# ScalarE's order in a top-k attention with a gated feed-forward: exponentials, evictions and sines by kind of slot

## The chip, the cores and the metric

The kernel runs on one core of one Trainium2 chip. The metric is the device time of one execution in microseconds (us). Before the change it is 1595.27 us, the median of three runs (1594.74 to 1595.98); the profiled execution has a span of 1596.1 us. Engines are named as in the profile: PE is TensorE (PEld its weight loads), DVE is VectorE, ACT is ScalarE, POOL is GpSimd, SP is SyncE.

## What is computed

An attention block that keeps the 32 largest scores of each row, and behind it a feed-forward with the gate h·cos(h). All of it is float32.

```python
# q, k, v: (B, H, S, D) = (8, 8, 576, 64);  w_in: (512, 2048);  w_out: (2048, 512)
scores = q @ k.T / sqrt(D)                       # per batch and head, 576 x 576
kth    = the 32nd largest of each row
scores = where(scores >= kth, scores, -1e9) - rowmax
attn   = exp(scores); attn /= attn.sum(-1) + 1e-9
x      = (attn @ v), heads side by side          # (4608, 512)
h      = x @ w_in
out    = (h * cos(h)) @ w_out                    # (4608, 512)
```

## The kernel before

The work is cut into 144 units: 36 tiles of 128 tokens, with four pairs of heads each. A tile of tokens with its four units feeds one block of the feed-forward. One pass of the main loop, a slot, starts the top-k of unit `u` and carries older units on: `w` is one slot older (its mask and exponentials), `x` two (normalised on POOL, split into halves and written to DRAM), `y` three (transposed by DMA), and `z` is a pair of units whose product with v is taken in every odd slot. Scores of the next units are made ahead: in most odd slots those of two units (`made` has two entries), in most even slots none. In a tile that lies across two batches (units 16 to 19, 52 to 55, 88 to 91 and 124 to 127) each unit's scores are made alone, one per slot.

```python
def slot(i, u, w, x, y, z):
    if x:
        reciprocal(x)              # DVE, waits for x's row sums
    if u:
        topk_first(u, w)           # DVE: two folds of u's scores, the last merges of w, round 0
        decode_second(2)
    if u:
        topk_round(u, 1); topk_round(u, 2); topk_round(u, 3)      # DVE
    if z:
        values(z)                  # PE: attn @ v of two units, into a PSUM tile
    made = scored.get(i, [])
    if not made or not z:
        feed(1)                    # PE: feed-forward tasks
    for m in made:
        scores(m)                  # PE
    if w:
        bounds(w)                  # ACT, waits for DVE's merges of w
        mask(w)                    # ACT, two Prelu over 128x576
    take_banks()                   # ACT: evictions of full feed-forward banks
    if z:
        take_values(z)             # ACT: xT, the feed-forward's input
    take_scores(units[i + 1])      # ACT: PSUM scores to SBUF
    if w:
        exponentials(w)            # ACT: two Exp with row sums, then den
    ...                            # loads, transposes(y)
    gate(1)                        # POOL: g = h * cos
    if x:
        normalise(x); split(x); write_halves(x)                   # POOL, SP
    feed(2)
    take_banks()
    ...
    reduce_first(); reduce_second()                               # POOL: argument of the cosine
    feed(3)
    sines(2)                       # ACT: cosine as a sine
```

Each engine carries its instructions out in this order. `feed(n)` puts up to `n` tasks of the feed-forward on PE, if the credit allows it. A task is a half of a bank with `w_in` (`ff1`) or a quarter of one with `w_out` (`ff2`: two of eight products into one bank); a block has eight of each. The kinds alternate two by two.

```python
ff["credit"] = min(ff["credit"] + 5.0 - 0.9 * len(scored.get(i, [])), 5.3)     # each slot
...
def open_bank():
    if ff["open"] + len(full) == 2:     # the feed-forward has two PSUM banks
        take_banks()
    ff["open"] += 1

def take_first(blk, g, mm, half):       # an ff1 bank: line 478
    nc.scalar.mul(out=g[:, half * 512 : half * 512 + 512], in_=mm, mul=INV_2PI)
    if half == 1:
        fresh.append([blk, g])

def take_second(blk, i, o):             # an ff2 bank: line 553
    ob = ffw.tile([P, DM], F32, tag="ob", name="ob")
    nc.scalar.mul(out=ob, in_=o, mul=2.0 * math.pi)
    nc.scalar.dma_start(out=out[row : row + P, :], in_=ob)
...
def sines(least):
    n = sum(c[3] < ff["now"] for c in waiting)          # reduced in an earlier slot
    if n == 0 or (n < least and waiting[0][3] + 2 > ff["now"]):
        return
    ...                                                  # Sin of each, line 523

def exponentials(u):                                     # line 334
    for j in range(2):
        nc.scalar.activation(out=s[:, j], in_=s[:, j], func=AF.Exp, bias=nd[:, j : j + 1],
                             scale=1.0, accum_out=den[:, j : j + 1])
    nc.scalar.activation(out=den, in_=den, func=AF.Identity, bias=eps, scale=1.0)
```

Exp and Sin need different activation tables, so a change from one to the other brings an ACT_TABLE_LOAD with it.

Of the kernel before, what the change touches and what calls it, by code (L numbers as in the profile page):

```python
# [31 lines left out]
def kernel(  # L32
# [52 lines left out]
    for i in range(DF // CW):  # L85
        w = consts.tile([P, NC, CW], F32, tag=f"w_in{i}", name=f"w_in{i}")
# [4 lines left out]
    for f in range(NF):  # L91
        w = consts.tile([P, DM], F32, tag=f"w_out{f}", name=f"w_out{f}")
# [38 lines left out]
    def decode_second(n):  # L131


        for _ in range(min(n, len(wq["second"]))):
            st, w = wq["second"].popleft()
            wi = w.bitcast(I32)
            nc.vector.tensor_scalar(out=w, in0=w, scalar1=2.0, scalar2=None, op0=ALU.max)
            nc.vector.tensor_scalar(
                out=wi, in0=wi, scalar1=3, scalar2=None, op0=ALU.logical_shift_left
            )  # L140
            wq["third"].append((st, w))
# [71 lines left out]
    def scores(u):  # L213
        sc = u["sc"] = ps.tile([P, 2, 512], F32, tag="sc", name="sc", bufs=2)
        for to, k0, k1 in ((sc, 0, SB), (sc_ends[u["n"] % 2], SB, S)):
            for j in range(2):
                d = slice(j * D, (j + 1) * D)
                for b, q0, rows, r0 in u["parts"]:
                    st = pairs[b, u["hp"]]
                    nc.tensor.matmul(  # L220
                        to[r0 : r0 + rows, j, 0 : k1 - k0],
                        st["q"][d, q0 : q0 + rows],
                        st["k"][d, k0:k1],
                        start=True,
                        stop=True,
                    )
# [30 lines left out]
    def topk_first(u, w):  # L257

        u["top"] = tops[u["n"] % len(tops)]
        merges = [merge_first, merge_second] if w and w["folds"] else []  # L260
        if u["folds"]:
            for op in (ALU.max, ALU.min):
                fold(u, op)
                if merges:
                    merges.pop(0)(w)
        else:
            u["rest"] = work.tile([P, 2, S], F32, tag="rest", name="rest", bufs=1)
        for merge in merges:
            merge(w)
        topk_round(u, 0)  # L270

    def topk_round(u, rnd):
        top, rest, lasts = u["top"], u["rest"], TOPK // 8 - 1
        end = TOPK - 1 - 8 * rnd
        at = top[:, :, end : end - 8 if rnd < lasts else None : -1, 0]
        if u["folds"]:
            search(at, rest[:, :, 0:HS], rest[:, :, 0:HS], rnd < lasts)
            if rnd < TOPK // 16:

                low = top[:, :, 1 + 8 * rnd : 9 + 8 * rnd, 1]  # L280
                search(low, rest[:, :, HS:S], rest[:, :, HS:S], rnd < TOPK // 16 - 1)
        else:
            search(at, u["s"] if rnd == 0 else rest, rest, rnd < lasts)
        if rnd == lasts:
            del u["rest"]
# [36 lines left out]
    def mask(u):  # L322

        s, nb = u["s"], u.pop("nb")
        for j in range(2):
            nc.scalar.activation(  # L326
                out=s[:, j], in_=s[:, j], func=AF.Prelu, bias=nb[:, j, 1:2], scale=SCALE, alpha=FAR
            )

    def exponentials(u):  # L330
        s, nd = u["s"], u.pop("nd")
        den = u["den"] = small.tile([P, 2], F32, tag="den", name="den")
        for j in range(2):
            nc.scalar.activation(  # L334
                out=s[:, j], in_=s[:, j], func=AF.Exp, bias=nd[:, j : j + 1], scale=1.0,
                accum_out=den[:, j : j + 1],
            )

        nc.scalar.activation(out=den, in_=den, func=AF.Identity, bias=eps, scale=1.0)  # L339

    def reciprocal(u):
        u["rden"] = small.tile([P, 2], F32, tag="rden", name="rden")
        nc.vector.reciprocal(u["rden"], u.pop("den"))  # L343
# [106 lines left out]
    def ff1(blk, i):  # L450
        w = blk["w"]
        nf = 256 // w
        part = i % 4
        if part == 0:
            blk["g"].append(ffw.tile([P, 1024], F32, tag="g", name="g", bufs=CHUNKS))
            ff["live"] += 1
        if part % 2 == 0:
            open_bank()
            blk["mm"] = ps.tile([P, 512], F32, tag="mm", name="mm", bufs=2)
        g, mm = blk["g"][-1], blk["mm"]  # L460
        for a in range(nf):
            f = i * nf + a
            at = (part % 2 * nf + a) * w
            for c in range(NC):
                nc.tensor.matmul(  # L465
                    mm[:, at : at + w],
                    w_in[f // FC][:, c, (f % FC) * P : (f % FC + 1) * P],
                    blk["xT"][:, c],
                    start=c == 0,
                    stop=c == NC - 1,  # L470
                )
        if part % 2 == 0:
            return
        ff["open"] -= 1
        full.append((take_first, blk, g, mm, part // 2))
# [6 lines left out]
    def take_banks():  # L482
        while full:
            take, *what = full.popleft()
            take(*what)
# [30 lines left out]
    def sines(least):  # L516

        n = sum(c[3] < ff["now"] for c in waiting)
        if n == 0 or (n < least and waiting[0][3] + 2 > ff["now"]):
            return  # L520
        for _ in range(n):
            blk, g, x, _, scale = waiting.popleft()
            nc.scalar.activation(out=x, in_=x, func=AF.Sin, bias=halfpi, scale=scale)  # L523
            sined.append((blk, g, x))
# [8 lines left out]
    def ff2(blk, i, f0):  # L533
        w = blk["w"]
        if f0 == 0:
            open_bank()
            blk["o"] = ps.tile([P, 512], F32, tag="mm", name="o2", bufs=2)
        o = blk["o"]
        per = 1024 // w
        for f in range(f0, f0 + 2):  # L540
            g = blk["g"][f // per]
            at = (f % per) * w + i * P
            nc.tensor.matmul(  # L543
                o, g[:, at : at + P], w_out[f], start=f == 0, stop=f == NF - 1
            )
        if f0 + 2 < NF:
            return
        ff["open"] -= 1
        full.append((take_second, blk, i, o))
# [25 lines left out]
    def feed(n):  # L575

        ff["tick"] += 1
        while n > 0 and ff["credit"] >= 1:
            for kind in (ff["kind"], 1 - ff["kind"]):
                if (can_first, can_second)[kind]():  # L580
                    break
            else:
                return
            if kind == 0:
                ff1(*first.popleft())
            else:
                ff2(*second.popleft())
            if kind != ff["kind"] or ff["half"]:
                ff["kind"], ff["half"] = 1 - kind, 0
            else:  # L590
                ff["half"] = 1
            n, ff["credit"] = n - 1, ff["credit"] - 1
# [8 lines left out]
    EARLY, LAST = 2 * NP, NU - NP  # L601
# [9 lines left out]
    for n in range(NP, len(order)):  # L611
        i = last[order[n - 5]] if n >= 5 else 0
        at_slot.setdefault(max(i, NP + 2), []).append((load_qk, *order[n]))
        i = last_values[order[n - 6]] if n >= 6 else 0
# [51 lines left out]
    def slot(i, u, w, x, y, z):  # L666
        if x:
            reciprocal(x)
        if u:
            topk_first(u, w)  # L670
            decode_second(2)
        if u:
            topk_round(u, 1)
            topk_round(u, 2)
            topk_round(u, 3)
        if z:
            values(z)
        made = scored.get(i, [])
        if not made or not z:
            feed(1)  # L680
        for m in made:
            scores(m)

        if w:
            bounds(w)
            mask(w)
        take_banks()
        if z:
            take_values(z)
        take_scores(units[i + 1])  # L690
        if w:
            exponentials(w)
        for load, b, hp in at_slot.get(i, []):
            load(b, hp)
        load_weights(2)
        if y:
            transposes(y)
        gate(1)
        if x:
            normalise(x)  # L700
            split(x)
            write_halves(x)
        feed(2)
        take_banks()
        decode_third()
        decode_first(2)
        reduce_first()
        reduce_second()
        feed(3)
        sines(2)  # L710

    def last_slot(i, u, w, x, y, z):
        if x:
# [48 lines left out]
    for i in range(NU + 1):  # L762
# [4 lines left out]
        u, w = (units[i - n] if 0 <= i - n < NU else None for n in range(2))  # L767
        x, y = (units[i - n] if EARLY <= i - n < LAST else None for n in range(2, 4))
        z = units[i - 5 : i - 3] if i % 2 and EARLY <= i - 5 < LAST else None
# [53 lines left out]
```

## Time and profile before

| engine | busy us | share of the span | instructions |
|---|---|---|---|
| PE | 1446.7 | 91% | 10360 |
| DVE | 1418.5 | 89% | 4689 |
| ACT | 1154.5 | 72% | 2322 |
| POOL | 1104.6 | 69% | 838 |

Two engines are near their whole span, and a third is far from it. The page's busy time is an average over a start (up to about 250 us, in which the weights are decoded), the long regular middle (to about 1475 us) and an end in which only the feed-forward is left: from 1500 us on DVE is busy 28.71 of 96 us, PE 91.67. In a list of waits, a line such as "DVE rden L343 <- ACT den L339" says which instruction stood idle and what let it go. A line of the timeline has the start, the duration, the engine, the line of code, the operation with output and input, the number of instructions merged, and in brackets the idle time ahead and its releaser.

### The profile page before, as it was taken

The numbers are of one execution on the slowest core, as the hardware profiler recorded it, in microseconds if no ns is written. First come the engines' busy times: TensorE is split into PE (matmuls) and PEld (weight loads), VectorE is DVE, ScalarE is ACT, GpSimd is POOL, SyncE is SP. The second block draws the span as 40 slices with busy tenths as digits, with TensorE's granted clock in tenths as the row PEclk, the third lists the DMA queues.
The fourth block names the chain that finished last, engine by engine and source line by source line (L and its number), as shares of the span: only waits on it lengthen the run. The fifth ranks groups of instructions, "written<-read, shape, count | busy, mean of one in ns | idle before, by whom it ended". The sixth has DMA issues, their size and how long they took to land.

```text
span 1596.1 us, 30173 instructions
## 1 busy us (share of the span) xinstructions
PE 1446.7 (91%) x10360; PEld 1041.4 (65%) x10360; DVE 1418.5 (89%) x4689; ACT 1154.5 (72%) x2322; POOL 1104.6 (69%) x838
## 2 busy tenths in 40 slices
PE   4568789999999999999999999999999999999999
PEld 2455467667676666766666666676766666767675
DVE  7999999998999998999999999999999999998821
ACT  7887666767777777777777777777777777777741
POOL 4687867866777777777777776777777767777610
PEclk6678799999999999999999999999999999999999
DMA  8423365545544465445564455644554445544300
GB/s 266 142 81 83 111 185 135 131 136 158 166 122 117 125 171 153 129 126 155 156 156 126 126 141 156 165 125 147 155 156 126 108 131 155 141 126 112 89 14 14
DMA packets 371753, 212.20 MB, mean 133 GB/s; under 512 B 321296, under 2 KB 337936, under 8 KB 371600
## 3 DMA queue, kind: packets, MB, share of 16 engines
q1 hardware_dynamic: 366192, 200.63, 45.7%
q10 hardware_dynamic: 5408, 9.65, 1.7%
q8 instruction: 81, 1.33, 0.3%
q14 instruction: 72, 0.59, 0.1%
HBM read 45.09 MB, written 87.29 MB: 83 GB/s over the span
## 4 chain that ended last, share of the span: by engine, by line
PE 39%; ACT 23%; DVE 20%; POOL 11%; issue 4%; DMA 2%; SPq 1%; DVEq 0%; ACTq 0%; POOLq 0%
PE mm L465 15%; PE o L543 12%; PE rim L408 6%; DVE top L304 6%; DVE rest L244 6%; ACT s L334 5%; DVE rest L307 5%; ACT s L326 5%; PE sc L220 4%; POOL g L530 3%; POOL halves L360 3%; ACT s L230 2%; ACT L334 2%; POOL s L348 2%; ACT nd L317 2%
## 5 line engine op out<-in xcount | busy, mean ns | idle before, releaser
L304 DVE MAX8 top<-rest 128x8 f32<-128x288 f32 (+1 forms) x1656 | 681.5, 460 | 0.0
L465 PE MATMUL mm<-xT,w_in 128*128 128x128 f32 x4608 | 586.7, 287 | 64.6 <-ACT g L478 56.6
L465 PEld LDWEIGHTS mm<-xT,w_in 128*128 128x128 f32 x4608 | 561.1, 201 | 122.2 <-ACT g L478 80.5
L543 PE MATMUL o<-w_out,g 128*128 128x512 f32 x1152 | 522.4, 596 | 6.1 <-POOL w_out L148 4.0
L307 DVE MATCH_REPLACE8 rest<-top,rest 128x288 f32<-128x288 f32 (+1 forms) x1104 | 494.9, 456 | 0.0
L543 PEld LDWEIGHTS o<-w_out,g 128*128 128x128 f32 x1152 | 208.8, 191 | 218.1 <-issue 208.0
L360 POOL COPY halves<-s 128x2304 uint16<-128x2304 uint16 x132 | 277.6, 2103 | 96.0 <-DMA rows<-halves 91.4
L348 POOL TENSOR_SCALAR s<-s,rden 128x576 f32<-128x576 f32 x288 | 212.0, 748 | 79.4 <-DVE rden L343 79.2
L334 ACT ACTIVATE s<-s,nd 128x576 f32<-128x576 f32 x288 | 221.1, 771 | 0.8
L504 POOL TENSOR_SCALAR x<-g 128x1024 f32<-128x1024 f32 x68 | 71.1, 1046 | 202.1 <-ACT g L478 202.1
L326 ACT ACTIVATE s<-s,nb 128x576 f32<-128x576 f32 x288 | 205.4, 760 | 0.0
L244 DVE TENSOR_TENSOR rest<-sc,s 128x576 f32<-128x576 f32 x264 | 198.6, 753 | 3.6 <-DVE rden L343 0.6
L408 PEld LDWEIGHTS rim<-pT,v 128*64 128x64 f32 x2560 | 136.4, 142 | 78.8 <-ACT nb L314 22.7
L408 PE MATMUL rim<-pT,v 128*64 128x128 f32 (+1 forms) x2560 | 164.7, 274 | 23.5 <-ACT pT L389 13.4
L530 POOL TENSOR_TENSOR g<-g,x 128x1024 f32<-128x1024 f32 x68 | 160.7, 2365 | 16.0 <-ACT x L523 16.0
L513 POOL TENSOR_TENSOR x<-g,x 128x1024 f32<-128x1024 f32 x68 | 161.3, 2372 | 5.7
L220 PE MATMUL sc<-k,q 64*128 64x448 f32 (+1 forms) x640 | 149.8, 591 | 14.5 <-DMA k<-in_k_dram 8.7
L314 ACT ACTIVATE nb<-top 128x4 f32<-128x4 f32 x144 | 29.3, 204 | 171.5 <-DVE top L297 171.0
L478 ACT ACTIVATE g<-mm 128x512 f32<-128x512 f32 x144 | 83.7, 583 | 84.4 <-PE mm L465 84.4
L230 ACT COPY s<-sc 128x896 f32<-128x896 f32 x144 | 129.3, 898 | 6.8 <-PE sc L220 6.8
L343 DVE RECIPROCAL rden<-den 128x2 f32<-128x2 f32 x144 | 22.5, 156 | 111.2 <-ACT den L339 110.0
L414 ACT COPY xT<-rim 128x256 f32<-128x256 f32 (+1 forms) x78 | 27.6, 354 | 119.6 <-PE rim L220 105.5
(55 smaller groups left out, 1339.1 us busy)
## 6 DMA issues: line engine op xcount, KB each, us to landing
rows<-halves SPq DMA_DIRECT2D x132, 576.0 KB, 3.2
out_dram<-ob ACTq DMA_DIRECT2D x36, 256.0 KB, 2.4
q<-in_q_dram SPq DMA_DIRECT2D x31, 288.0 KB, 3.1
st<-in_moe_w_in_dram SPq DMA_DIRECT2D x16, 512.0 KB, 5.4
v<-in_v_dram SPq DMA_DIRECT2D x32, 256.0 KB, 3.2
st<-in_moe_w_out_dram SPq DMA_DIRECT2D x16, 512.0 KB, 3.5
k<-in_k_dram SPq DMA_DIRECT2D x31, 144.0 KB, 3.4
k<-in_k_dram SPq DMA_DIRECT2D x32, 128.0 KB, 4.0
```

The lines of the kernel that those rows point to most:

```text
L220: nc.tensor.matmul(to[r0 : r0 + rows, j, 0 : k1 - k0], st["q"][d, q0 : q0 + rows], st["k"][d, k0:k1], start=True, stop=True,)
L244: nc.vector.tensor_tensor(out=u["rest"][:, :, i * HS : (i + 1) * HS], in0=sc[:, :, 0:HS], in1=s[:, :, HS:S], op=op,)
L304: nc.vector.max(to[:, j], src[:, j])
L307: nc.vector.match_replace(rest[:, j], to[:, j], src[:, j], NEG)
L326: nc.scalar.activation(out=s[:, j], in_=s[:, j], func=AF.Prelu, bias=nb[:, j, 1:2], scale=SCALE, alpha=FAR)
L334: nc.scalar.activation(out=s[:, j], in_=s[:, j], func=AF.Exp, bias=nd[:, j : j + 1], scale=1.0, accum_out=den[:, j : j + 1],)
L348: nc.gpsimd.tensor_scalar(out=s[:, j], in0=s[:, j], scalar1=rden[:, j : j + 1], scalar2=1.0, op0=ALU.mult, op1=ALU.mult,)
L360: nc.gpsimd.tensor_copy(out=halves, in_=s.rearrange("p (k h) -> p h k", h=2))
L408: nc.tensor.matmul(o[d, to], lhsT, rhs, start=c == 0, stop=c == NT)
L465: nc.tensor.matmul(mm[:, at : at + w], w_in[f // FC][:, c, (f % FC) * P : (f % FC + 1) * P], blk["xT"][:, c], start=c == 0, stop=c == NC - 1,)
L530: eng.tensor_tensor(out=g, in0=g, in1=x, op=ALU.mult)
L543: nc.tensor.matmul(o, g[:, at : at + P], w_out[f], start=f == 0, stop=f == NF - 1)
```

## The change

It changes the order in which ACT takes its work, by the kind of slot. In an odd slot in which scores of two units are made (`late`), the exponentials come right behind the mask, ahead of the evictions of the feed-forward's bank, of xT and of the scores. In a slot in which no scores are made, a full bank is taken first of all, before the bounds that wait for DVE. Sines are issued in odd slots only, as soon as one is ready; in even slots only near the start and the end. And a `late` slot ends with one task of the feed-forward at most, not three. It is meant to keep DVE from waiting for row sums behind work that waits for PE, and PE from waiting for a bank behind work that waits for DVE.

```diff
         for m in made:
             scores(m)
 
+
+        late = z and len(made) == 2
+        if not made:
+            take_banks()
         if w:
             bounds(w)
             mask(w)
+        if w and late:
+            exponentials(w)
         take_banks()
         if z:
             take_values(z)
         take_scores(units[i + 1])
-        if w:
+        if w and not late:
             exponentials(w)
         for load, b, hp in at_slot.get(i, []):
             load(b, hp)
@@
         reduce_first()
         reduce_second()
-        feed(3)
-        sines(2)
+        feed(1 if late else 3)
+        if i % 2:
+            sines(1)
+        elif i < EARLY + 8 or i > LAST - 2:
+            sines(2)
```

`EARLY` is 8 and `LAST` is 140.

## Prediction

> **What bounds the kernel now.** I read the page first: busy times, then the costliest groups. No engine is the bound alone.
>
> ```profile
> PE 1446.7 (91%) x10360; PEld 1041.4 (65%) x10360; DVE 1418.5 (89%) x4689; ACT 1154.5 (72%) x2322; POOL 1104.6 (69%) x838
> ...
> PE 39%; ACT 23%; DVE 20%; POOL 11%; issue 4%; DMA 2%; SPq 1%; DVEq 0%; ACTq 0%; POOLq 0%
> ...
> L465 PE MATMUL mm<-xT,w_in 128*128 128x128 f32 x4608 | 586.7, 287 | 64.6 <-ACT g L478 56.6
> ```
>
> The chain that ended last changes engines all the time, and ACT, busy only 72%, holds 23% of it: it carries the waits from one near-full engine to the other. So the list of waits comes next, for 400 to 1450 us (the regular middle).
>
> ```profile
> ACT nb L314 <- DVE top L297: 121.2, 77, 1.9
> ACT xT L414 <- PE rim L220: 83.0, 48, 3.1
> ...
> DVE rden L343 <- ACT den L339: 72.8, 28, 3.8
> PEld mm L465 <- ACT g L478: 66.5, 26, 2.8
> ACT g L478 <- PE mm L465: 49.2, 26, 2.6
> PE mm L465 <- ACT g L478: 46.8, 26, 1.9
> ```
>
> In these 1050 us are some 26 blocks of four slots, and there are 28 DVE waits (2.6 us each) and 26 PE waits (1.8 us each): one of each per block. Next, DVE's timeline, from which I take each slot's start (its reciprocal).
>
> ```profile
> 882.03 0.17 DVE L343 RECIPROCAL rden<-den 128x2 f32<-128x2 f32 x1 [2.00 <-ACT den L339]
> ...
> 891.44 0.15 DVE L343 RECIPROCAL rden<-den 128x2 f32<-128x2 f32 x1
> ...
> 901.07 0.17 DVE L343 RECIPROCAL rden<-den 128x2 f32<-128x2 f32 x1
> ...
> 910.48 0.14 DVE L343 RECIPROCAL rden<-den 128x2 f32<-128x2 f32 x1
> ...
> 923.69 0.17 DVE L343 RECIPROCAL rden<-den 128x2 f32<-128x2 f32 x1 [3.63 <-ACT den L339]
> ```
>
> Without the wait the four slots are 9.41 + 9.63 + 9.41 + (13.21 − 3.63 = 9.58) = 38.03 us: DVE's floor per block. The stall is 3.63 us in one block and 2.00 in the next, so blocks take 41.66 and 40.03 us, 40.85 on average. Last, the timeline around it:
>
> ```profile
> 904.81 0.57 ACT L478 ACTIVATE g<-mm 128x512 f32<-128x512 f32 x1
> ...
> 905.44 5.47 PE L465 MATMUL mm<-xT,w_in 128*128 128x128 f32 x32 [1.93 <-ACT g L478]
> ...
> 918.87 0.37 ACT L414 COPY xT<-rim 128x256 f32<-128x256 f32 x1 [2.93 <-PE rim L220]
> ...
> 920.34 1.28 ACT L334 ACT_TABLE_LOAD   x1
> ...
> 923.30 0.29 ACT L339 ACTIVATE den<-den,eps 128x2 f32<-128x2 f32 x1
> ```
>
> This is a ring. In the even slot from 901.07, ACT waits for DVE's merges until 902.86, runs bounds and mask, and only then (904.81) empties a bank that was full since about 900.1 (its matmuls began at 896.68 and took 3.39); PE stands 1.93 us for it. PE is then late with values and scores of the odd slot (from 910.48), so ACT gets xT at 918.87, the scores after it, and the exponentials, with a table load, end at 923.6. DVE, ready at 920.06, waits for them. Each engine's wait is the other's cause.
>
> The two stall lengths differ by 1.63 us, and so does the matmul group behind PE's wait: 5.47 us here, 3.84 in the other block (at 865.41). Asking for 3.4-us stretches gives granted clocks below 1:
>
> ```profile
> 904.70:908.10 3.40, 2.66 (x16) 2.66 (x17) 3.40 (x14) 3.37 (x9) 1.83 (x1) 0.73 0.80 181
> 908.10:911.50 3.40, 3.40 (x20) 3.02 (x20) 3.36 (x13) 0.76 (x2) 0.00 (x0) 0.77 0.44 171
> ```
>
> (the clock is the figure behind the five engines' busy times, ahead of the DMA share). So in every second block PE's wait also costs 1.63 us of slower clock.
>
> PE's floor: from one block's values (851.27) to the next (891.30) are 40.03 us; less the waits, 2.1 at the bank (the group ahead, at 859.88, lasts 3.43 to the next start where no wait follows; 865.41 − 859.88 − 3.43) and 0.2 at xT, leaves 37.7 us. Both floors are within 0.4 us of each other, 3 us below the block's 40.85.
>
> **What the Trainium skill says.** "PSUM — Partial Sum Buffer", Engine vs sequencer instructions: the queues of ScalarE, VectorE and GpSimd are strictly first in, first out. The trace agrees: the eviction at 904.81 sat behind a mask that waited 1.88 us for DVE. "ScalarE: Activation LUTs", What ACT_TABLE_LOAD costs: 1283 ns per load, any set, plus a drain to about 2.66 us. The trace has 1283 ns for 66 Sin and 65 Exp loads, but no added drain: load at 920.34, Exp at 921.64, so I count 1.30 us. "TensorE: Matmul & The Clock Gate", What's actually happening: the clock halves after an idle window of about 3.4 us that runs freely. The trace shows the halving, but a 1.93-us wait is enough in every second block, and the 0.81-us ones (groups at 578.22 and 947.12, both 3.84 us) cost none.
>
> **The change part by part.** First the tasks' order, by following the counters of the code. A pair of slots needs 8 tasks. Credit is 5 − 1.8 = 3.2 in the odd slot and 5 in the even one, so 3 and 5 tasks run there before and after alike; the smaller feed(1) takes nothing away, since credit allows three in the odd slot anyway. Written as PE's order (v values, s scores, 1 = w_in task, 2 = w_out task), before: v s s 11 22 11 22, in both pairs. After: pair I v s s 11 2 | 2 11 22, pair II v s s 22 1 | 1 11 22, the bar being the slot's edge. Two tasks fewer are left behind the last slot, 28 instead of 30.
>
> *A full bank first, even slots.* In pair I the bank taken is the finished w_out bank and no w_in bank is missing: PE's 2.1 us are gone. In pair II four w_in tasks follow one another, with the other bank held open by w_out; PE must wait out one eviction: 0.20 us to its start (910.74 to 910.94), 0.60 of it, 0.06 back (904.81 + 0.57 to 905.44): 0.86 us. PE per block: 37.7 + 0.86 = 38.55 us. Waits this short showed no slower clock, so the 1.63 every second block (0.8 us on average) goes too.
>
> *Exponentials ahead, odd slots.* Let PE start the values L us after DVE's slot. Before, den ended at L + 2.3 (values) + 2.15 (scores) + 1.6 (xT, scores to SBUF) + 1.3 (table) + 2.2 (two Exp, den) = L + 9.6, against a slot of 9.6: any lateness of PE stalled DVE. (In the slot from 910.48 the values began at 914.27, L = 3.8, and the stall was 3.63.) After, with Sin now at the end of odd slots, the Exp of the odd slot finds its table still loaded: bounds at 1.9, mask to 3.85, den at about 6.0, whatever PE does. What DVE needs next is the copied scores, at the later of 7.4 and L + 6.0; PE may be 3.6 us late. No DVE stall at the end of odd slots.
>
> *Single sines.* 72 sines run with 66 loads now, nearly all single already: the count of loads stays, and their place moves. The Exp load comes in the even slot: the bank's eviction starts at L + 11.8 from the odd slot's start (values and scores 4.5, then four tasks of 1.8), ends by L + 12.75 with the output's DMA issue (855.24 to 856.23), then bounds and mask 1.95, scores 1.05, table 1.3, two Exp and den 2.0: L + 19.05, against 19.02 for a pair of DVE slots. ACT has just no slack here: DVE waits L if PE is late by L. But PE's own pairs are 18.8 us (872.61 to 891.30 now, a pair without a wait) and the remaining 19.7, so L swings between about −0.2 and +0.4, and the pair's time is set by PE: 38.55 us per block, DVE's 38.03 hidden beside it. I take 38.7 for unmodelled semaphores.
>
> *Sum.* From 249.63 (slot 19) to 1475.91 us are 120 slots, 30 blocks. Three of them straddle two batches; there the old order holds in both slots, and two evictions are forced inside a slot, one behind exponentials with a table load (about 3 us of PE). I give these no gain. 27 × (40.85 − 38.7) = 58 us. Two tasks fewer at the end, about 1.8 us each, where PE runs alone: 4 us. 1595.3 − 58 − 4 = 1533 us.
>
> **Rivals.** (a) *ACT's even slot becomes the bound*: an eviction that waits for PE now stands ahead of bounds, mask and a table load. For: no slack, as computed; DVE's present wait is turned from the odd to the even slot's end. Against: PE's wait it replaces is longer. If it costs 1 us per pair, blocks take 39.7 to 40 and the time is 1560 to 1570. (b) *POOL's chain slips*: sines come later, the gate stands in order ahead of the normalising, and POOL's argument reductions start behind the even slot's last eviction. Its 69% busy, and about 2.7 us left until the transposed rows are needed by my count, speak against; if rows come late by 1 to 2 us a pair, nothing is gained: 1590 or more. (c) *Both rings open fully* and DVE's 38.03 us is the block even across straddling tiles: 30 × 2.82 + 4 = 89 us less, 1507.
>
> **Range and chances.** Rival (c) is nearly the floor: low 1512. Half-way into (a), with straddling blocks that lose, is 1568: high. Faster by over 2% means below 1563.4; I expect 3.9% and give it 0.80. Within 2%: 0.17, mostly (a). Slower by 2% needs (b) in earnest: 0.03.
>
> **What would show it.** Right: the wait of DVE's reciprocal for den falls below about 30 us in all; PE's wait for g falls to some 0.7 us, once per block; no 5.47-us groups and a mean clock above 0.947; Exp loads in even slots only; regular blocks of 38.4 to 38.9 us. Wrong: DVE waiting for den in every odd slot's beginning (a), PE's values waiting for pT from DMA (b), or a new PE wait for g over 1 us at the four w_in tasks in a row.

## The result, and the profile after

The changed kernel takes 1540.97 us (median; 1539.62 to 1542.78), against 1595.01 us before on the same chip: a ratio of 0.9661, with a 95% interval of 0.9645 to 0.9678. The medians differ by 54.0 us; the profiled execution has a span of 1537.8 us, 58.3 less than the one before.

Busy times, the chain that ended last and the w_in matmuls, from the page of the changed kernel:

```profile
PE 1419.5 (92%) x10360; PEld 1018.8 (66%) x10360; DVE 1416.3 (92%) x4689; ACT 1158.8 (75%) x2326; POOL 1105.3 (72%) x838
...
PE 80%; ACT 8%; DVE 4%; POOL 3%; DMA 2%; SPq 1%; issue 1%; ACTq 0%; POOLq 0%; DVEq 0%
...
L465 PE MATMUL mm<-xT,w_in 128*128 128x128 f32 x4608 | 554.5, 279 | 32.8 <-ACT g L478 32.8
```

The chain no longer changes hands: PE has 80% of it, where it had 39%. Its idle time ahead of the w_in matmuls has halved from 64.6 us, and they are busy 32.2 us less for the same count, because fewer run at a reduced clock: 31.2 us of the difference lie between slots 20 and 140, where the granted clock has risen from 0.98 to 1.00 (in the whole span from 0.947 to 0.963).

The list of waits of the changed kernel, 400 to 1400 us:

```profile
...
ACT g L478 <- PE mm L465: 82.3, 51, 3.3
POOL g L530 <- ACT x L523: 62.9, 24, 6.2
...
DVE rden L343 <- ACT den L339: 29.2, 31, 4.1
PE mm L465 <- ACT g L478: 28.7, 32, 2.9
...
ACT xT L414 <- PE rim L220: 15.4, 5, 6.3
```

Each line has the total in us, the number of waits and the longest. DVE's wait for den has fallen from 72.8 us to 29.2, PE's for g from 46.8 to 28.7 (the earlier figures are for 1050 us, these for 1000). In their place ACT waits longer for PE's bank, 82.3 us after 49.2, and POOL for the sine; both have the time, and all their idle time together is less than before. One regular block, from DVE's timeline and PE's:

```profile
859.97 0.17 DVE L343 RECIPROCAL rden<-den 128x2 f32<-128x2 f32 x1 [0.29 <-ACT den L339]
...
869.38 0.15 DVE L343 RECIPROCAL rden<-den 128x2 f32<-128x2 f32 x1
878.90 0.15 DVE L343 RECIPROCAL rden<-den 128x2 f32<-128x2 f32 x1
888.40 0.15 DVE L343 RECIPROCAL rden<-den 128x2 f32<-128x2 f32 x1
898.28 0.17 DVE L343 RECIPROCAL rden<-den 128x2 f32<-128x2 f32 x1 [0.27 <-ACT den L339]
```

```profile
867.38 3.73 PE L465 MATMUL mm<-xT,w_in 128*128 128x128 f32 x32
871.80 3.84 PE L465 MATMUL mm<-xT,w_in 128*128 128x128 f32 x32 [0.69 <-ACT g L478]
875.48 3.60 PE L543 MATMUL o<-w_out,g 128*128 128x512 f32 x8
```

The block takes 898.28 − 859.97 = 38.31 us (40.85 on average before). Four w_in tasks stand in a row, and PE waits 0.69 us between them for the eviction, once per block; the group behind it lasts 3.84 us, where 5.47 us stood in every second block before.

From slot 20 (the one the prediction calls slot 19, at 249.63 us before and 244.32 after) to slot 140 the changed kernel takes 1177.2 us, where the kernel before took 1226.3: 49.1 us. The start gives another 5.3, the end (from slot 140 on, 120.2 and 116.3) 3.9; together the 58.3 us of the two spans. But the first four slots behind slot 20 take 43.11 us for 38.09 before, since DVE waits 2.28 us for copied scores (at 246.74) and 1.55 and 1.30 us for den (at 257.69 and 278.01): by slot 24 the lead of the start has shrunk from 5.3 to 0.3 us.

### The profile page after: what moved, and what is told of

It reads as the page before. It is cut to its first block, busy times and chain, and to the rows that moved or that the text cites. A ratio compares the mean times of both kernels' runs of the same rounds, so it can differ in the third digit from the quotient of the medians.

```text
span 1537.8 us, 30197 instructions
## 1 busy us (share of the span) xinstructions
PE 1419.5 (92%) x10360; PEld 1018.8 (66%) x10360; DVE 1416.3 (92%) x4689; ACT 1158.8 (75%) x2326; POOL 1105.3 (72%) x838
## 4 chain that ended last, share of the span: by engine, by line
PE 80%; ACT 8%; DVE 4%; POOL 3%; DMA 2%; SPq 1%; issue 1%; ACTq 0%; POOLq 0%; DVEq 0%
PE mm L465 30%; PE o L543 30%; PE rim L408 10%; PE sc L220 7%; PE rim L220 2%; ACT g L478 2%; DVE top L304 2%; ACT s L334 1%; DVE rest L307 1%; DMA pT<-rows 1%; ACT s L326 1%; DVE w_out L138 1%; POOL s L348 1%; ACT st L127 1%; ACT s L230 1%
## 5 line engine op out<-in xcount | busy, mean ns | idle before, releaser
L465 PEld LDWEIGHTS mm<-xT,w_in 128*128 128x128 f32 x4608 | 538.3, 194 | 80.1 <-ACT g L478 41.0
L465 PE MATMUL mm<-xT,w_in 128*128 128x128 f32 x4608 | 554.5, 279 | 32.8 <-ACT g L478 32.8
L543 PE MATMUL o<-w_out,g 128*128 128x512 f32 x1152 | 529.4, 602 | 12.7 <-POOL g L530 6.8
L478 ACT ACTIVATE g<-mm 128x512 f32<-128x512 f32 x144 | 84.5, 588 | 122.3 <-PE mm L465 122.3
L220 PEld LDWEIGHTS rim<-k,q 64*128 64x128 f32 (+1 forms) x640 | 57.2, 182 | 58.9 <-issue 53.9
```

Source lines behind the costliest of these rows:

```text
L220: nc.tensor.matmul(to[r0 : r0 + rows, j, 0 : k1 - k0], st["q"][d, q0 : q0 + rows], st["k"][d, k0:k1], start=True, stop=True,)
L465: nc.tensor.matmul(mm[:, at : at + w], w_in[f // FC][:, c, (f % FC) * P : (f % FC + 1) * P], blk["xT"][:, c], start=c == 0, stop=c == NC - 1,)
L543: nc.tensor.matmul(o, g[:, at : at + P], w_out[f], start=f == 0, stop=f == NF - 1)
```

## The experiments

Two theories were set against each other. **One ring**: DVE's late merges delay ACT's mask, which delays the bank, which delays PE, which delays scores and exponentials, which delay DVE; a cut anywhere frees all. **Two waits**, each with its own price, each removed by its own part. All times are medians; ratios are to the kernel before on the same chip. "Block" is the median length of four slots between slots 20 and 140, from the starts of DVE's reciprocals in the profile.

| kernel | us | ratio, 95% interval | block us |
|---|---|---|---|
| before | 1595.0 | 1 | 40.0 and 41.7 by turns |
| the whole change | 1541.0 | 0.9661, 0.9645 to 0.9678 | 38.36 |
| e1: exponentials ahead, alone | 1536.6 | 0.9621, 0.9605 to 0.9637 | 38.75 |
| e2: a full bank first, alone | 1520.0 | 0.9524, 0.9507 to 0.9541 | 38.04 |
| e3: both of these | 1540.8 | 0.9645, 0.9625 to 0.9666 | 38.72 |
| e4: the change without exponentials ahead | 1541.2 | 0.9650, 0.9635 to 0.9664 | 38.38 |
| e5: the change without the bank first | 1602.0 | 1.0031, 1.0018 to 1.0043 | 41.51 |
| e6: the change without single sines | 1526.4 | 0.9555, 0.9531 to 0.9579 | 38.06 |
| e7: the change without feed(1) | 1790.0 | 1.1205, 1.1184 to 1.1225 | 47.63 |
| e8: the change in every tile | 1520.1 | 0.9514, 0.9495 to 0.9533 | 38.36 |
| e9: the bank first in every tile, alone | 1518.4 | 0.9500, 0.9487 to 0.9513 | 38.04 |
| e10: e9, exponentials ahead at the start | 1516.7 | 0.9498, 0.9485 to 0.9511 | 38.04 |
| e11: exponentials ahead and feed(1) | 1521.2 | 0.9525, 0.9508 to 0.9542 | 38.05 |

### One part alone: e1 and e2

e1, against the kernel before:

```diff
+        late = z and len(made) == 2
         if w:
             bounds(w)
             mask(w)
+        if w and late:
+            exponentials(w)
         take_banks()
 ...
-        if w:
+        if w and not late:
             exponentials(w)
```

> The kernel before with one part: exponentials ahead of the evictions in slots with two units' scores. The bank's eviction in even slots, the sines and feed(3) stay as before. Theory 1 (one ring, any cut opens it): with DVE free of PE's lateness, PE may run 2 us late, and then its bank has been emptied when it gets there; both waits go, regular blocks take 38.1 to 38.6 us instead of 40.85, 1530 to 1540 us in all. Theory 2 (two waits, each with its own price): DVE's wait for den goes, PE's 1.93 us for g and its slower clock stay, blocks of about 40.3 us, 1575 to 1585 us.

e2, against the kernel before:

```diff
+        if not made:
+            take_banks()
         if w:
             bounds(w)
             mask(w)
```

> The kernel before with one part: a full bank first in slots in which no scores are made. Theory 1 (one ring): without the 2 us at the bank PE is never late enough for DVE to wait for den more than 0.3 us a block; regular blocks 38.1 to 38.6 us, 1530 to 1540 us. Theory 2 (each wait its own price): PE's wait goes, DVE's 2 us or more per block stay, 1575 to 1585 us.

Measured: 1536.6 and 1520.0 us. The theory of one ring holds for both, and e2, two lines of the change, is below the range expected and 21 us faster than the whole. The waits of PE and then of DVE in e2, 400 to 1400 us:

```profile
PE mm L465 <- ACT xT L414: 10.9, 20, 1.4
PE mm L465 <- ACT g L478: 2.4, 3, 0.8
```

```profile
DVE rden L343 <- ACT den L339: 8.2, 7, 1.8
```

With PE's wait for g gone, DVE's wait for den is nearly gone as well, though the exponentials are where they were. Regular blocks take 38.04 us, DVE's own 38.03, and the chain that ended last in e2 says who is the bound now:

```profile
DVE 55%; PE 14%; ACT 13%; POOL 9%; issue 4%; DMA 3%; SPq 1%; ACTq 0%; POOLq 0%; DVEq 0%
```

e1 opens the ring from the other side (PE's wait for g falls to 2.4 us there too) but stays 0.7 us per block above the floor. Its waits, of PE and then of DVE:

```profile
PE mm L465 <- ACT xT L414: 26.2, 23, 2.2
```

```profile
DVE rest L244 <- ACT s L231: 17.1, 22, 1.1
```

In the odd slot the exponentials, with their table load, now stand ahead of xT and the scores. In one odd slot per block xT is what PE needs next: the first w_in task is of the block that this xT completes. PE runs the few matmuls whose input is older and waits 1.06 us or a little more; DVE waits up to 1.1 us for the copied scores.

### Both, and each left out: e3, e4, e5

e3 is e1 and e2 together; e4 and e5 are the changed kernel with the exponentials behind the scores' eviction again, and with the bank behind the mask again.

> The kernel before with exponentials ahead and a full bank first; sines and feed(3) as before. The tasks' order stays the old one (11 22 11 22), so there is no row of four w_in tasks and no 0.69-us wait. Theory 1 (ring): regular blocks at DVE's floor, 38.0 to 38.3 us, 1525 to 1538 us, at least as fast as the whole change; sines and feed(1) are then no part of the gain. Rival (the Exp load in odd slots is what costs): DVE waits for den again, 1550 to 1570 us.

> The changed kernel, with the exponentials behind the scores' eviction again in every slot. Theory 1: the ring stays cut at the bank; DVE's odd slots end at L + 8.3 us without a table load, so no new wait; 1535 to 1550 us. Theory 2: DVE's wait for den comes back with 1 to 2 us per block, 1565 to 1590 us.

> The changed kernel, with the bank taken behind the mask again in slots without scores. Theory 1: PE falls back by about 1.5 us, which DVE now bears, and waits no longer than the 0.7 us it waits with the change; 1535 to 1550 us. Theory 2: PE waits 2 us for its bank in each block and loses clock in every second one, 1570 to 1590 us.

e3, 1540.8 us, misses its expectation: it is slower than e2 by 21 us and no faster than e1. DVE does not wait for den, as the rival had it (8.9 us from 400 to 1400 us); PE waits for xT, 25.4 us in 23 times, as in e1. Exponentials ahead add this cost to a ring that the bank has opened already. e4, 1541.2 us, equals the whole change: with single sines and feed(1) the exponentials' place makes no difference that is seen, in either direction.

e5, 1602.0 us, is against the theory as I had put it: a cut at the exponentials should have been enough. Pieces of e5's timeline, ACT, then DVE, then a w_in group of PE half a block earlier:

```profile
1050.72 0.60 ACT L478 ACTIVATE g<-mm 128x512 f32<-128x512 f32 x1 [2.30 <-PE mm L465]
1051.34 1.28 ACT L523 ACT_TABLE_LOAD   x1
1052.63 1.15 ACT L523 ACTIVATE x<-x,halfpi 128x1024 f32<-128x1024 f32 x1
1053.69 0.19 ACT L314 ACTIVATE nb<-top 128x4 f32<-128x4 f32 x1
...
1057.82 1.28 ACT L334 ACT_TABLE_LOAD   x1
...
1060.77 0.29 ACT L339 ACTIVATE den<-den,eps 128x2 f32<-128x2 f32 x1
```

```profile
1061.16 0.17 DVE L343 RECIPROCAL rden<-den 128x2 f32<-128x2 f32 x1 [3.32 <-ACT den L339]
```

```profile
1033.54 5.46 PE L465 MATMUL mm<-xT,w_in 128*128 128x128 f32 x32 [2.09 <-ACT g L478]
```

The odd slot's end is free, but the wait has moved to the even slot. ACT waits for PE's bank (1050.72), then comes the sine, only then the bounds of the even slot, the mask, and an Exp table load; DVE gets den 3.32 us late. PE in turn waits 2.1 to 2.25 us between its four w_in tasks, since that bank is behind a mask. The ring is closed again, through the sine. e11 puts this to the test: e5 with sines(2) in every slot, so exponentials ahead and feed(1) alone.

> The kernel before with exponentials ahead and feed(1), without the bank and without the single sines. Exponentials alone gave 1536.6 us, but exponentials, sines and feed(1) without the bank 1602. If the sine at the end of odd slots, with its Exp load in the even slot, is what closes the ring again: the ring stays open here, and the order 22 1 | 1 22 11 hides xT, so blocks of 38.0 to 38.7 us and 1522 to 1540 us. If feed(1) with its later tasks closes it: 1590 to 1605 us.

1521.2 us, blocks of 38.05: without the single sines the ring stays open. With feed(1), PE takes two w_out tasks ahead of w_in in three of four odd slots (with e1's feed(3), w_in always came first), and it has no wait for xT left in the list, the cost of e1: the same exponentials, 15 us less.

### The sines and the feed: e6 and e7

Both against the changed kernel:

```diff
 # e6                                  # e7
-        if i % 2:                     -        feed(1 if late else 3)
-            sines(1)                  +        feed(3)
-        elif ...:
-            sines(2)
+        sines(2)
```

> The changed kernel with sines(2) in every slot as before. By the counters the tasks' order becomes 22 1 | 1 22 11, the 0.69-us wait of PE goes, but four more tasks are left at the end (32 against 28, 7 us). If sines only move a table load: 1532 to 1545 us. If their place is part of the gain (the Exp load back on DVE's path in odd slots): 1555 to 1570 us.

> The changed kernel with feed(3) at the end of every slot. As the prediction put it, feed(1) takes nothing away, since credit allows three tasks in the odd slot anyway: 1541 us, within 4. Rival, by following the counters again: without it an even slot starved of tasks hands credit on, the next odd slot takes a fourth task and forces an eviction in 28 more slots, up to 0.9 us of PE each: 1550 to 1570 us.

e6, 1526.4 us, is below both ranges: the single sines are a loss, 15 us in this kernel. PE's wait for g between w_in tasks falls from 28.7 to 3.2 us (400 to 1400 us) and regular blocks reach DVE's floor, 38.06 us for 38.36. Yet most of the gain lies elsewhere: of 23.0 us between slots 20 and 140, 15.9 come from the eight slots around each of the three tiles across two batches (231.5 us for 247.3). Some is given back behind slot 140, 122.3 us against 116.3.

e7, 1790.0 us, is far outside both expectations. Three pieces of its timeline, ACT, POOL and PE:

```profile
913.27 0.60 ACT L478 ACTIVATE g<-mm 128x512 f32<-128x512 f32 x1 [4.02 <-PE mm L465]
...
915.18 1.15 ACT L523 ACTIVATE x<-x,halfpi 128x1024 f32<-128x1024 f32 x1
```

```profile
916.41 2.35 POOL L530 TENSOR_TENSOR g<-g,x 128x1024 f32<-128x1024 f32 x1 [12.74 <-ACT x L523]
```

```profile
942.80 7.37 PE L543 MATMUL o<-w_out,g 128*128 128x512 f32 x10 [5.40 <-POOL g L530]
```

The rival's counting was right in kind: credit is handed on, and a further w_in task in the odd slot forces an eviction. But its price is not 0.9 us of PE. ACT waits 4.02 us for that bank ahead of the sine, POOL waits 12.74 us for the sine with the normalising of DVE's next unit behind it, and the starved even slot puts three w_out tasks right behind their own gate, so PE waits 5.40 us once per block.

### Every tile: e8, e9, e10

e8 is the changed kernel with `late = bool(z)` and `if not z: take_banks()`; e9 is the kernel before with `if not z: take_banks()` ahead of the bounds and nothing else; e10 is e9 with the exponentials ahead in slots below 20 only.

> The changed kernel with the new order and feed(1) in every odd slot that has a pair for values, and the bank first in every other slot, so also in the tiles that lie across two batches. If the old order there and its forced evictions are what costs (two blocks of 81.3 to 83.5 us around each of three tiles, against 76.7 elsewhere): 1521 to 1528 us, and the 2.93-us waits for g are gone. If those tiles are slow in themselves (scores made one unit at a time, in the same slot that needs them): 1536 to 1541 us.

> The kernel before with nothing but a full bank first in every slot without values, the tiles across two batches too. With the bank alone, a full bank first where no scores are made, the blocks of those three tiles took 40.8, 40.9 and 40.0 us against 38.04 elsewhere, and DVE still waited 1.0 to 1.8 us for den there. If the eviction behind the mask is the cause there too: 7 us less, 1511 to 1515 us, every block at 38.0 to 38.5. If scores made in the same slot are the cause: 1519 to 1521 us.

> As the bank first in every slot without values, and the exponentials ahead only in the slots with two units' scores before slot 20. At the start of slot 20 DVE waits 3.25 us for den with the bank alone, and not so with exponentials ahead. If that wait is a loss of its own: 3 to 4 us less than with the bank in every tile, 1507 to 1512 us. If it is made up for later (PE is late there anyway): the same time within 1 us.

In the changed kernel, around slot 52, a tile across two batches (ACT's timeline, then PE's):

```profile
563.89 0.77 ACT L334 ACTIVATE s<-s,nd 128x576 f32<-128x576 f32 x1
...
565.75 0.58 ACT L478 ACTIVATE g<-mm 128x512 f32<-128x512 f32 x1
```

```profile
566.38 2.05 PE L465 MATMUL mm<-xT,w_in 128*128 128x128 f32 x16 [2.93 <-ACT g L478]
```

The forced eviction stands behind the exponentials, and PE waits 2.93 us; it does so once in each of these tiles. e8 takes 1520.1 us, 21 less than the change; the eight slots around each of these tiles fall from 81.28, 82.56 and 83.49 us to 76.38, 76.36 and 76.39, and from 400 to 1400 us no wait of PE for g is above 0.7 us. So the cost there is the old order, but only together with the single sines: of the kernels with regular blocks of 38.0 to 38.8 us and the old order in these tiles, those with single sines (the change, e4) take 247.3 and 248.2 us for the three times eight slots, those without (e1, e2, e3, e6, e11) 231.4 to 237.4. e9 takes 1518.4 us and misses its range: the eight slots fall from 78.89, 78.95 and 78.07 to 78.07, 77.97 and 77.20 us, 2.7 us in all where 7 were expected. Since e8 has no loss in these tiles though scores are made in the same slot there as well, these are not the cause either. e11, which moves neither the bank nor the exponentials in these tiles but has another order of tasks, takes 76.04, 79.36 and 76.04 us there: this speaks for the tasks' order in two of the three, and does not show it. e10, 1516.7 us, starts slot 20 at 246.43 us instead of 249.66, but 2.0 us of that are lost again by slot 140, 1.9 of them in the first four slots, and the intervals of e9 and e10 lie almost on each other: undecided. e2, e6 and e8 to e11 are all clearly faster than both kernels; e9, two lines, is as fast as any.

## Why the prediction was right, and where it was wrong

The time, 1533 us, was 8 us low, inside its range, and the ring that it read from the profile is what the change opens: e2 and e1 show it from two sides. Its account of the parts is another matter: that each of them helps is not so, and that the sum came out so near is in part luck. Point by point:

- *A full bank first*: right, and more than its share. In this set it is the one part without which nothing is gained (e5), and alone it gains more than all (e2); e1 and e11 gain without it. PE's loss in a row of four w_in tasks was worked out as 0.86 us, and is that: 0.69 us idle, and from start to start 871.80 − 867.38 = 4.42 us where such a group without a wait takes 3.57 (890.60 to 894.17), 0.85 lost. Groups of 5.47 us are gone from regular blocks.
- *Exponentials ahead*: the step failed as a part of the gain. The sum of L + 9.6 against 9.6 was true of a PE that is 2 us late; with the bank first PE is not late, and den came in time from the old place (e2, e4). What I left out is what stands behind the exponentials then: xT, which PE needs at once when the first task is of the new block (e1, e3).
- *Single sines*: the count of loads stayed (68 Sin loads for 66) and the Exp load went to the even slot, right. "ACT has just no slack here" was right: DVE waits 0.25 to 0.33 us there in regular blocks. That the part is a loss (e6), I did not draw from it. In regular blocks the loss is 0.3 us; whether the sines' place or the row of four w_in tasks makes it, no run separates. Rival (a) was real, but small so long as the bank is first, except in the tiles across two batches.
- *feed(1) takes nothing away*: wrong twice. In the regular slots of the old sequence credit is the limit, but near the start feed(1) holds tasks back: behind the values at 233 us PE runs two w_in tasks fewer in e11 than in e1, and from 314 us on e11 has w_out first in three pairs of slots out of four. With single sines an even slot is starved and hands credit on, and the same line decides between 1541 and 1790 us (e7). The order of the tasks that I counted for the change itself is the one in the trace.
- *Straddling tiles*: mis-sized. I gave no gain to three blocks; it was six, the eight slots around each tile, 247.3 us against 246.6 before. e8 shows that this loss goes with the old order, e6 that it goes with the single sines as well.
- *Regular blocks*: 24 are left where I counted 27, and they took 929.8 us for 979.7 before. The first is the slow one behind slot 20 (43.11 us for 38.09); the other 23 took 38.55 each for 40.94, a little better than the 38.7 predicted.
- *The end*: 3.9 us for 4. *The start*: 5.3 us that I did not count; exponentials ahead remove most of DVE's wait of 3.62 us at slot 20 (e10 shows 3.2), and the first block takes 5.0 us back.
- *The sum*, in the profiled executions: 23 × 2.39 − 0.7 − 5.0 + 5.3 + 3.9 = 58 us, for 62 predicted. Better regular blocks stand against three more blocks without a gain, and the start against the first block: these offset each other by luck.
- Of the signs named, DVE's wait for den in all is 53.3 us, not below 30. From 400 to 1400 us it is 29.2, and some 22 of these lie in the straddling tiles and the blocks right behind them; the rest of the 53.3 lies nearer the start and the end.

## What to carry to other kernels

Where two engines near their limit wait for each other through a third, the waits are not to be added up: look for the one instruction whose place closes the ring, move that alone, and measure before moving more. An eviction whose bank has long been full is better placed ahead of a wait for another engine, as e2 shows here; a long job put ahead in an in-order queue delays all that stood there before it, so list what is behind it and who needs that next. And a set of parts that is tuned together can hide that some only mend what others break: without feed(1) the changed kernel takes 1790 us (e7), yet without the single sines as well nothing needs it, as e3 shows with 1541 us.

## What the runs showed of the hardware

The reduced clock again followed PE's longer idle times and not the shorter ones. In e5, from 400 to 1400 us, 12 of 17 whole groups behind waits of 2.09 to 2.25 us took 5.33 to 5.47 us and the other five 3.84. In e1 the waits for xT of 1.06 to 1.54 us slowed no group, and one of 1.67 us did (4.58 us for 24 matmuls, which take 2.94 otherwise). Whole groups behind 0.69 us took 3.84. The Trainium skill, "TensorE: Matmul & The Clock Gate" (What's actually happening), has the clock halve after at least one idle window of about 3.4 us; here about half of that was at times enough.

Where the wait falls decides it, and this is why only every second block lost clock before. From 300 to 1450 us every reduced stretch of the kernel before lasts 3.41 us, and all begin whole multiples of 3.41 us apart. The wait that ends at 905.44 lies wholly in one stretch of this grid, 902.86 to 906.27: PE is idle for 1.92 us of it, 56%, and the clock in the next one is 0.50. The wait that ends at 865.41 sticks 0.1 us out of its stretch, 861.90 to 865.31: 1.83 us are idle, 54%, and the clock stays at 1.00. From 300 to 1400 us of the kernel before and of e5, a step to the reduced clock follows every stretch with 56% idle or more (15 and 16) and none with less. The limit is known only roughly, since the ends of matmuls are modelled: in e1 a stretch with 49% brought a step, in the changed kernel one with 56% brought none.
